# Retention attention and a GELU MLP on one core: first loads reordered, first weight conversions moved behind the chunks' steps, last product split by tokens

## The chip, the cores and the metric

The kernel runs on one core of one Trainium2 chip. The metric is device time in microseconds (us) of one execution. Engines are named as in the profile: PE is TensorE (matmul), PEld its weight loads, DVE is VectorE, ACT is ScalarE, POOL is GpSimd, SP is SyncE, which here only issues DMAs. "L198" is line 198 of the kernel.

## The reference

```python
# retention attention: batch 4, heads 8, 768 steps, head_dim 64
for t in range(S):
    state = gamma[None, :, None, None] * state + np.einsum('bhd,bhe->bhde', k[:, :, t], v[:, :, t])
    y[:, :, t] = scale * np.einsum('bhd,bhde->bhe', q[:, :, t], state)
# bridge: x is y as 3072 tokens x 512
h = x @ w_in                                   # 512 -> 2048
g = h * (1.0 / (1.0 + np.exp(-1.702 * h)))     # quick GELU
return (g @ w_out).astype(np.float32)          # 2048 -> 512
```

The two weight matrices are float64. They reach the chip as raw 64-bit words, and the kernel itself turns them into float32.

## The kernel before

The sequence is cut into 24 chunks of 128 tokens. A chunk goes through three steps: `turn` (transpose q and k on TensorE, copy the result out of PSUM on ScalarE), `attend` (scores on TensorE, mask on VectorE) and `finish` (output and state on TensorE, scaling into `X` on VectorE, decay of the state on GpSimd). The order of TensorE's instructions is the program's. A scheduler sets the order on the other engines, but every engine takes its own instructions one after the other: in the profile, ScalarE began L188 at 40.41 behind L308 at 39.92, as in the program.

Weights come in pieces of 512 KB, and two pieces make the block of one product. `narrow()` converts weights: one pass of ScalarE, then six passes of VectorE. Its first two calls convert one piece each, which together are the first block; every later call converts the two pieces of a whole block.

```python
    def narrow():
        ...
        tc.keep_in_program_order(act.activation(m, hi.bitcast(F32), AF.Abs, scale=2.0 ** 16))          # L188
        tc.keep_in_program_order(dve.tensor_scalar(m, m, F64_MOST * 2.0 ** 16, F64_LEAST * 2.0 ** 16,
                                                   op0=ALU.min, op1=ALU.max))                          # L189
        dve.tensor_scalar(mu, mu, 3, None, op0=ALU.logical_shift_left)                                 # L191
        dve.scalar_tensor_tensor(hi, hi, 0x80000000, mu, op0=ALU.bitwise_and, op1=ALU.bitwise_or)      # L192
        dve.tensor_scalar(mu, hi, 0xFF800000, None, op0=ALU.bitwise_and)                               # L193
        dve.scalar_tensor_tensor(lo.bitcast(F32), lo, 2.0 ** -52, m, op0=ALU.mult, op1=ALU.mult)       # L194
        ...
        dve.tensor_add(w, hi, lo)                                                                      # L198
```

`up0(half, p)` is one product of the MLP's first layer: 8 matmuls into one PSUM tile (16 matmul records in the profile, two for each), then a sigmoid on ScalarE and a multiplication on VectorE. `up0(0, 0)`, `up0(0, 1)` and `up0(0, 2)` are called the first, second and third product below. The third has one more product of the same form directly behind it, with nothing between, so the profile shows the two as one stretch, and I time them as one.

```python
    def hidden(g, h):
        act.activation(s, h, AF.Sigmoid, scale=1.702)       # L308
        ...
            dve.tensor_mul(g, h[:, i], s[:, i])             # L310

    def up0(half, p, tag):
        h = ps.tile([P, 2, TH], F32, name="ph", tag=tag)
        for ab in range(2):
            for c in range(4):
                w = W1[:, p, 2 * ab + c // 2, c % 2, :]
                pe.matmul(h[:, ab], w, X[:, 2 * half + c // 2, c % 2, :], ...)      # L329
        ...  # hidden(...)
```

The start of the program:

```python
    load(0)
    ...
    first = const.tile([P, 1], F32, name="first")
    dve.memset(first, 0.0)
    act.activation(first, first, AF.Sigmoid)     # brings ScalarE's table in early
    fetch()                                      # first weight piece
    load(1)
    fetch()
    ...
    for j in range(CB):                          # CB = 4
        attend(j)
        narrow()
        if j == 1:
            narrow()
        turn(j + 1)
        if j == 0:
            for _ in range(2):
                fetch()
        if j < CB - 1:
            attend(None, j)                      # finish(j)
        else:
            attend(j + 1, j)
        if j:
            up0(0, j - 1, "x")
    ...                                          # the long up stage: 13 products more, narrow() after every other
```

The last product of the last block of tokens is 16 matmuls into one PSUM tile (32 records), an add on VectorE (L423) and one store of 256 KB (L424).

Of the kernel before, what the change touches and what calls it, by code (L numbers as in the profile page):

```python
# [9 lines left out]
F32 = mybir.dt.float32  # L10
U32 = mybir.dt.uint32
AF = mybir.ActivationFunctionType
ALU = mybir.AluOpType
P = 128
# [14 lines left out]
def kernel(  # L29
# [29 lines left out]
    pe, act, dve, pool, sp = nc.tensor, nc.scalar, nc.vector, nc.gpsimd, nc.sync  # L59
# [11 lines left out]
    NB = NCH // CB  # L71
    NFF = DFF // P
    NP = NFF // 2
    C4 = 32
    EH = DM // 2
# [13 lines left out]
    W2 = const.tile([P, 7, NP, EH], F32, name="W2")  # L89
# [16 lines left out]
    def load(j, what="qkv"):  # L106


        b, c = divmod(j, NC)
        rows = slice(c * P, (c + 1) * P)  # L110

        def plain(name, src, tag, bufs, pairs=False, engine=sp):
            t = two.tile([P, H, D], F32, name=name + "_in", tag=tag, bufs=bufs)
            QKV[name, j] = t
            src = src[b, :, rows, :].rearrange("h p d -> p h d")
            if pairs:
                for i in range(2):
                    engine.dma_start(t[:, i:H:2, :], src[:, i * HP:(i + 1) * HP, :])
            else:
                sp.dma_start(t, src)  # L120

        if j < 2 * CB:
            if "q" in what:
                plain("q", q, "q_sq", 2, True)
                plain("kn", k, "k_sq", 2, True, sp if j else act)
        elif "q" in what:
            for name, src in (("q", q), ("k", k)):
                t = two.tile([P, HP, P // C4, C4], F32, name=name + "_sq")
                for r0 in range(0, P, C4):
                    d0 = r0 % D  # L130
                    for hp in range(HP):
                        tc.keep_in_program_order(sp.dma_start(
                            t[r0:r0 + C4, hp],
                            src[b, hp + HP * (r0 // D), rows, d0:d0 + C4].rearrange("(s p) d -> p s d", p=C4)))
                QKV[name, j] = t
        if "v" in what:
            if j >= 2 * CB and c < NC - 1:
                plain("kn", k, "kn", 1)
            plain("v", v, "v", 2)
# [24 lines left out]
    def narrow():  # L164


        i = narrowed[0]
        if i == len(SRC):
            return
        n = 1 if i < 2 else 2  # L170
        narrowed[0] = i + n
        p, h = i // 2 % NP, i % 2

        if i < 2:
            m = W1[:, 1, 2 * h:2 * h + 2].rearrange("p s c f -> p (s c f)")
            w = W1[:, 0, h:4:2].rearrange("p ab c f -> p c ab f")
        elif i < NFF:
            m = W1[:, p, 0:4].rearrange("p s c f -> p (s c f)")
            w = W1[:, p, 0:4].rearrange("p (ab h) c f -> p (h c) ab f", ab=2)
        else:  # L180
            m = w = W2[:, 0:4, p]
        x = raw(i, n).rearrange("p (n two) -> p n two", two=2)
        lo, hi = x[:, :, 0], x[:, :, 1]
        if i >= NFF:
            lo, hi = [t.rearrange("p (s e) -> p s e", s=4) for t in (lo, hi)]
        mu = m.bitcast(U32)
# [8 lines that stand above are left out]
        lo, hi = lo.bitcast(F32), hi.bitcast(F32)  # L195
        if i < NFF:
            lo, hi = [t.rearrange("p (c ab f) -> p c ab f", ab=2, f=P) for t in (lo, hi)]
        dve.tensor_add(w, hi, lo)  # L198
        for _ in range(n):
            fetch()  # L200
# [119 lines left out]
    def g1(m, p, s):  # L320
        return g(m, p // 2 * 2, s)[:, p % 2]
# [7 lines that stand above are left out]
                pe.matmul(h[:, ab], w, X[:, 2 * half + c // 2, c % 2, :], start=(ab == 0 and c == 0), stop=(c == 3),  # L329
                          skip_group_check=True)  # L330
        if half == 0:
            hidden(W1[:, p, 4:6].rearrange("p s c f -> p s (c f)"), h)
        else:
            hidden([(g1(0, p, 2 + i), i) for i in range(2)], h)
# [77 lines left out]
    def down(m):  # L412

        acc, kept = {}, {}
        rows = out[m * BT:(m + 1) * BT, :].rearrange("(h t p) (e c) -> h e p t c", h=2, p=P, c=EH)

        def keep(name, tag, src):
            kept[name] = one.tile([P, 2, EH], F32, name=name, tag=tag)
            act.activation(kept[name], src, AF.Copy)  # L419

        def put(th, e, a, b):
            o = two.tile([P, 2, EH], F32, name="o")
            dve.tensor_add(o, a, b)  # L423
            (pool if m < NB - 1 else act).dma_start(rows[th, e], o)  # L424

        def part(key, sa, sb, new, last, d, then):
            if d == 0 and new:
                acc[key] = ps.tile([P, 2, EH], F32, name="pd", tag=key[0])
            p0 = acc[key]
            for p in range(2 * d, 2 * d + 2):  # L430
                for n in range(2):
                    pe.matmul(p0[:, n, :], g1(m, p, sa)[:, n * P:(n + 1) * P], W2[:, sb, p, :],  # L432
                              start=(new and p == 0 and n == 0), stop=(last and p == NP - 1), skip_group_check=True)
            if d == NP // 2 - 1:
                then(p0)

        def then_p5(y):
            kept["t"] = one.tile([P, 2, EH], F32, name="t", tag="s1")
            dve.tensor_add(kept["t"], y, kept["u"])

        def then_p7(x):
            keep("vv", "s3", x)
            put(1, 0, acc["y1"], kept["vv"])
            put(1, 1, acc["y2"], kept["vv"])

        P_ = [("x", 0, 0, True, False, lambda x: keep("p1", "s1", x)),
              ("y0", 1, 2, True, True, lambda y: put(0, 0, y, kept["p1"])),
              ("y1", 3, 1, True, True, lambda y: None),
              ("x", 0, 5, False, False, lambda x: keep("u", "s2", x)),
              ("y2", 3, 4, True, True, then_p5),  # L450
              ("x", 2, 6, False, True, then_p7),
              ("x2", 1, 3, True, True, lambda y: put(0, 1, y, kept["t"]))]
        todo = []
        for n, (key, sa, sb, new, last, then) in enumerate(P_):
            for d in range(NP // 2):
                def unit(key=key, sa=sa, sb=sb, new=new, last=last, d=d, then=then, n=n):
                    part(key, sa, sb, new, last, d, then)
                    if n == 2:
                        sums_g(m, 2 * d)
                todo.append(unit)  # L460
        return todo


    load(0)
    make_identity(nc, ident)
    pool.dma_start(cold, col_decay[:, 0:2 * H])
    for i in range(2):
        pool.dma_start(rowd[i * D:(i + 1) * D], bass.AP(tensor=row_decay.tensor, offset=row_decay.offset + i * P,
                                                        ap=[[0, D], [2 * P, HP], [1, P]]))

    first = const.tile([P, 1], F32, name="first")
    dve.memset(first, 0.0)
    act.activation(first, first, AF.Sigmoid)
    fetch()
    load(1)
    fetch()
    idle = ps.tile([P, HP, P], F32, name="idle", tag="x")

# [14 lines left out]
    def chunks(first, last):  # L493

        return [s for j in range(first, last + 1)
                for s in (lambda j=j: turn(j), lambda j=j: attend(j, j - 1))]
# [12 lines left out]
        fetch()  # L509
    for j in range(CB):  # L510
        attend(j)
        narrow()
        if j == 1:
            narrow()
        turn(j + 1)
        if j == 0:
# [3 lines that stand above are left out]
            attend(None, j)  # L520
        else:
            attend(j + 1, j)
        if j:
            up0(0, j - 1, "x")
    between = chunks(CB + 1, 2 * CB - 1) + [lambda: attend(None, 2 * CB - 1)]
    for n, unit in enumerate([(1, p) for p in range(3)] + [(half, p) for p in range(3, NP) for half in range(2)]):
        up0(*unit, "xxyx"[n % 4])
# [81 lines left out]
```

## Time and profile before

| | before |
|---|---|
| median of the first 3 runs | 703.62 us (702.62 to 704.25) |
| span of the profiled run, mean clock | 701.9 us, 0.991 |
| TensorE busy | 686.3 us |
| idle of TensorE in all | 15.6 us |

The prediction shows the slices, the timelines of start and end and the clock windows. Read from windows of 0.1 us, the granted clock of this profile fell from 1.00 to 0.50 at 10.28, 23.93 and 34.17 us and rose again at 13.69, 27.34 and 37.58. Each half-speed stretch took 3.41 us, and the six times lie multiples of 3.41 us apart, within 0.02. The windows of about 3.4 us are laid on these times, and by phase the prediction means where a gap lies against them. The view it does not show is the table of waits of TensorE (engine, waiting group, what it waited for: us in total, times, longest):

```profile
PE py L284 <- DVE G L263: 2.5, 3, 1.3
PE pt L225 <- DMA q_in<-in_q_dram: 2.5, 3, 2.0
...
PE ph L329 <- DVE W L198: 0.9, 1, 0.9
...
PE pt L225 <- DMA kn_in<-in_k_dram: 0.3, 1, 0.3
```

L198 is the last pass of a conversion; the up products (L329) waited for it once, for 0.9 us. Conversions were ahead of their use.

### The profile page before, as it was taken

The page shows a single profiled execution, that of the slowest core. Times are in us where ns is not written, and L with a number is a line of the kernel's source. Part 1 is how long each engine was busy: PE and PEld are TensorE (multiplying, and loading weights), DVE is VectorE, ACT ScalarE, POOL GpSimd, SP SyncE. Part 2 cuts the span into 40 slices and gives each one's busy share as a digit, 9 for nine tenths or more (in the row PEclk, how much of TensorE's full clock was granted, in tenths as well). Part 3 has the DMA queues.
Part 4 walks back from the last instruction along what each step waited for, and adds up shares of the span by engine and source line. Part 5 has one row for each costly group of instructions (what it writes and reads, how often), then busy time and mean ns, then how long its engine had stood idle before and what let it go on. Part 6 is the DMA issues. An engine that isn't in the chain of part 4 may idle for free.

```text
span 701.9 us, 11046 instructions
## 1 busy us (share of the span) xinstructions
PE 686.3 (98%) x4493; PEld 572.5 (82%) x4493; DVE 361.5 (52%) x521; ACT 125.8 (18%) x197; POOL 129.7 (18%) x126
## 2 busy tenths in 40 slices
PE   6799999999999999999999999999999999999997
PEld 5588885447888888888888888888888888888886
DVE  3989889993711822443742453453345362344241
ACT  3213333311000001331000332000333000233000
POOL 4221000000466404000324000132200143000030
PEclk9899999999999999999999999999999999999999
DMA  9884343421130224200334300324300210000001
GB/s 230 264 231 133 135 136 135 138 35 28 28 65 27 63 46 103 46 1 15 72 62 91 65 1 8 72 45 90 74 0 3 60 30 13 34 1 1 15 1 45
DMA packets 138754, 46.36 MB, mean 66 GB/s; under 512 B 130176, under 2 KB 131216, under 8 KB 138704
## 3 DMA queue, kind: packets, MB, share of 16 engines
q1 hardware_dynamic: 134704, 38.84, 23.2%
q0 software_dynamic: 1856, 5.52, 2.1%
q10 hardware_dynamic: 2144, 1.31, 0.6%
q8 instruction: 35, 0.57, 0.3%
q14 instruction: 15, 0.12, 0.1%
HBM read 39.33 MB, written 6.29 MB: 65 GB/s over the span
## 4 chain that ended last, share of the span: by engine, by line
PE 93%; DVE 5%; DMA 1%; ACT 0%; SPq 0%; issue 0%; ACTq 0%
PE pd L432 39%; PE px L381 16%; PE py L381 12%; PE ph L329 8%; PE ph L342 8%; PE py L284 4%; PE pa L257 3%; PE py L292 1%; PE py L282 1%; DMA q_in<-in_q_dram 1%; DVE W L371 1%; DVE G L371 1%; PE pt L225 1%; DVE G L372 1%; DVE W L372 1%; DVE W L198 0%
## 5 line engine op out<-in xcount | busy, mean ns | idle before, releaser
L432 PE MATMUL pd<-W,G 128*128 128x256 f32 x1120 | 247.4, 381 | 0.4 <-DVE G L372 0.3
L432 PEld LDWEIGHTS pd<-W,G 128*128 128x128 f32 x1120 | 211.4, 190 | 30.4 <-DVE G L372 1.2
L381 PE MATMUL px<-X,W 128*128 128x256 f32 x512 | 119.0, 379 | 0.0
L381 PEld LDWEIGHTS px<-X,W 128*128 128x128 f32 x512 | 97.3, 190 | 13.2
L381 PE MATMUL py<-X,W 128*128 128x256 f32 x384 | 90.7, 379 | 0.0
L381 PEld LDWEIGHTS py<-X,W 128*128 128x128 f32 x384 | 73.0, 190 | 9.9
L263 DVE TENSOR_TENSOR at<-pa,mask 128x512 f32<-128x512 f32 x32 | 21.7, 686 | 79.6 <-PE py L284 70.8
L329 PE MATMUL ph<-X,W 128*128 128x256 f32 x256 | 60.9, 397 | 1.6 <-DVE W L198 0.9
L329 PEld LDWEIGHTS ph<-X,W 128*128 128x128 f32 x256 | 49.9, 199 | 9.7 <-DVE W L198 1.3
L342 PE MATMUL ph<-W,W 128*128 128x512 f32 x128 | 55.1, 592 | 0.0
L244 POOL TENSOR_TENSOR kd<-kn_in,cold 128x512 f32<-128x512 f32 x13 | 13.5, 1038 | 208.9 <-PE py L292 179.4
L342 PEld LDWEIGHTS ph<-W,W 128*128 128x128 f32 x128 | 24.3, 190 | 30.2 <-issue 29.2
L373 POOL TENSOR_TENSOR G<-G 128x512 f32<-128x512 f32 x20 | 29.5, 1480 | 95.0 <-DVE G L372 92.2
L310 DVE TENSOR_TENSOR G<-G,sg 128x512 f32<-128x512 f32 x48 | 33.0, 688 | 13.7 <-ACT sg L308 13.7
L308 ACT ACTIVATE sg<-G 128x512 f32<-128x512 f32 x48 | 30.2, 630 | 51.0 <-DVE G L391 30.7
L424 POOL DMA_DIRECT2D out_dram<-o x20 | 14.9, 744 | 128.5 <-DVE o L423 128.5
L308 ACT ACTIVATE sg<-ph 128x512 f32<-128x512 f32 x32 | 19.1, 597 | 100.6 <-PE ph L329 49.8
L432 PE MATMUL pd<-W,W 128*128 128x256 f32 x160 | 35.8, 381 | 0.4 <-DVE W L372 0.3
L432 PEld LDWEIGHTS pd<-W,W 128*128 128x128 f32 x160 | 30.2, 190 | 5.7 <-DVE W L372 1.2
L391 DVE TENSOR_TENSOR G<-py,p 128x512 f32<-128x512 f32 x16 | 11.1, 691 | 37.8 <-PE py L381 37.8
L419 ACT ACTIVATE u<-pd 128x512 f32<-128x512 f32 x6 | 3.6, 597 | 148.5 <-PE pd L432 148.5
L423 DVE TENSOR_TENSOR o<-pd,vv 128x512 f32<-128x512 f32 x12 | 7.7, 686 | 35.6 <-ACT vv L419 35.6
(102 smaller groups left out, 655.9 us busy)
## 6 DMA issues: line engine op xcount, KB each, us to landing
v_in<-in_v_dram SPq DMA_DIRECT2D x24, 256.0 KB, 3.5
W<-in_moe_w_in_dram SPq DMA_DIRECT2D x12, 512.0 KB, 4.8
W<-in_moe_w_out_dram SPq DMA_DIRECT2D x10, 512.0 KB, 3.7
out_dram<-o POOLq DMA_DIRECT2D x20, 256.0 KB, 2.7
q_sq<-in_q_dram SPq DMA_DIRECT2D x256, 16.0 KB, 1.7
k_sq<-in_k_dram SPq DMA_DIRECT2D x256, 16.0 KB, 1.7
kn_in<-in_k_dram SPq DMA_DIRECT2D x13, 256.0 KB, 3.2
G<-in_moe_w_out_dram SPq DMA_DIRECT2D x6, 512.0 KB, 3.7
```

Source lines behind the costliest of these rows:

```text
L257: pe.matmul(p[t, i, hp, :], kt[r, hp, t], qt[r, hp, :], start=True, stop=True)
L263: dve.tensor_mul(AT[j][:, i], p[:, i], mask[:, i])
L284: pe.matmul(out, vn[:, HP * r + s, :], a[:, r, s, :], start=(not c and s < 2), stop=(s >= 2), skip_group_check=True)
L308: act.activation(s, h, AF.Sigmoid, scale=1.702)
L310: dve.tensor_mul(g, h[:, i], s[:, i])
L329: pe.matmul(h[:, ab], w, X[:, 2 * half + c // 2, c % 2, :], start=(ab == 0 and c == 0), stop=(c == 3), skip_group_check=True)
L342: pe.matmul(h, w, X1[:, c // 2:4:2, c % 2, :], start=(c == 0), stop=(c == 3))
L371: dve.tensor_sub(a[2], a[0], a[2])
L373: pool.tensor_sub(a[1], a[1], a[0])
L381: pe.matmul(acc[:, u, :], W1[:, 2 * d + u, sa, c, :], X[:, sb, c, :], start=(start and u == 0 and c == 0), stop=(stop and c == 1), skip_gr ...
L424: (pool if m < NB - 1 else act).dma_start(rows[th, e], o)
L432: pe.matmul(p0[:, n, :], g1(m, p, sa)[:, n * P:(n + 1) * P], W2[:, sb, p, :], start=(new and p == 0 and n == 0), stop=(last and p == NP - ...
```

## The change

The intent is to shorten start and end. q and k of chunk 1 are requested ahead of the first weight piece. ScalarE's table is loaded before k. The first conversions stand behind the chunks' steps, so that the attention work comes first. The last product is made by halves of tokens, so that the add and store of the first half run under the second.

```diff
+        def last_product(n):
+            if n == 0:
+                acc["x2"] = ps.tile([P, 2, EH], F32, name="pd", tag="x")
+            y = acc["x2"][:, n, :]
+            for p in range(NP):
+                pe.matmul(y, g1(m, p, 1)[:, n * P:(n + 1) * P], W2[:, 3, p, :], start=(n == 0 and p == 0), ...)
+            o = two.tile([P, EH], F32, name="o")
+            dve.tensor_add(o, y, kept["t"][:, n, :])
+            (act, sp)[n].dma_start(rows[0, 1][:, n, :], o)
 ...
+        if m == NB - 1:
+            todo[-NP // 2:] = [lambda n=n: last_product(n) for n in range(2)]
 ...
+    first = const.tile([P, 1], F32, name="first")
+    dve.memset(first, 0.0)
+    act.activation(first, first, AF.Sigmoid)
     load(0)
 ...
-    first = const.tile([P, 1], F32, name="first")
-    dve.memset(first, 0.0)
-    act.activation(first, first, AF.Sigmoid)
+    load(1, "qk")
     fetch()
-    load(1)
+    load(1, "v")
     fetch()
 ...
         attend(j)
-        narrow()
-        if j == 1:
+        if j:
             narrow()
         turn(j + 1)
 ...
         if j:
             up0(0, j - 1, "x")
+        else:
+            narrow()
```

More of the change, by code (lines that the diff above doesn't have):

```diff
@@ L435, in part @@
                 then(p0)
+        def last_product(n):
[3 more added lines that the diff above has]
+            for p in range(NP):
+                pe.matmul(y, g1(m, p, 1)[:, n * P:(n + 1) * P], W2[:, 3, p, :], start=(n == 0 and p == 0),
+                          stop=(p == NP - 1), skip_group_check=True)
+            o = two.tile([P, EH], F32, name="o")
+            dve.tensor_add(o, y, kept["t"][:, n, :])
+            (act, sp)[n].dma_start(rows[0, 1][:, n, :], o)
         def then_p5(y):
```

## The prediction

> **What bounds the kernel now.** I read the busy shares and slices first, then the waits of TensorE, then the timeline of the start and of the end, and last TensorE's busy time in windows of 3.4 us. The slices of the page:
>
> ```profile
> PE   6799999999999999999999999999999999999997
> DVE  3989889993711822443742453453345362344241
> PEclk9899999999999999999999999999999999999999
> ```
>
> TensorE (PE) works 686.3 of 701.9 us. What it lacks is in the first three slices and the last one: the page has no other gap. So only two places can pay, the first 45 us and the tail, and both are what the change touches. The whole sum of idle time is 15.6 us (2.2%), and VectorE (DVE) is as full as TensorE in the start. The timeline of all engines, start:
>
> ```profile
> 10.79 1.09 PE L225 MATMUL pt<-ident,q_in 128*128 128x128 f32 x4 [1.99 <-DMA q_in<-in_q_dram]
> ...
> 22.88 1.17 ACT L188 ACTIVATE W<-W 128x1024 f32<-128x1024 f32 x1 [4.54 <-DVE W L194]
> ...
> 23.63 4.54 PE L329 MATMUL ph<-X,W 128*128 128x256 f32 x12 [0.86 <-DVE W L198]
> ...
> 31.18 1.22 DVE L198 TENSOR_TENSOR W<-W 128x1024 f32<-128x1024 f32 x1
> ...
> 34.80 5.08 PE L329 MATMUL ph<-X,W 128*128 128x256 f32 x16
> ...
> 39.92 0.60 ACT L308 ACTIVATE sg<-ph 128x512 f32<-128x512 f32 x1 [8.95 <-PE ph L329]
> 40.41 1.17 ACT L188 ACTIVATE W<-W 128x1024 f32<-128x1024 f32 x1
> 40.55 0.69 DVE L310 TENSOR_TENSOR W<-ph,sg 128x512 f32<-128x512 f32 x1 [0.49 <-ACT sg L308]
> ...
> 48.48 1.22 DVE L198 TENSOR_TENSOR W<-W 128x1024 f32<-128x1024 f32 x1
> ```
>
> To be seen: the first wait of note, 1.99 us, is for chunk 1's q. Each weight piece is converted by one ScalarE pass (L188) and six VectorE passes (L189 to L198). The conversion of the second block starts at 22.88, **before** TensorE has run the first up product (23.63 to 28.1), and its last pass ends at 32.40, ahead of the second product at 34.80. Conversions run one block ahead of their use. The lines from 39.92 on show a whole block's conversion started *behind* a product: that took from 39.81 (product over) to 49.70 (48.48 + 1.22), 9.89 us.
>
> TensorE in windows of about 3.4 us (columns: window and length, PE, PEld, DVE, ACT, POOL busy, clock, DMA share, GB/s):
>
> ```profile
> 20.60:24.00 3.40, 1.76 (x13) 1.13 (x9) 2.81 (x6) 1.12 (x1) 0.14 (x1) 0.99 0.95 267
> 24.00:27.40 3.40, 3.40 (x10) 2.69 (x9) 3.25 (x3) 0.05 (x1) 1.93 (x2) 0.51 1.01 319
> ```
>
> Where TensorE was busy 1.76 of 3.4 us, the next window ran at a clock of 0.51. The same happened after 1.54 (6.9 to 10.3) and after 1.61 (30.8 to 34.2), not after 2.60 (41.0 to 44.4). Some 1.7 us of idle in a window is thus followed by a half-speed window, which costs up to another 1.7 us.
>
> The tail of the timeline:
>
> ```profile
> 684.75 12.90 PE L432 MATMUL pd<-W,G 128*128 128x256 f32 x59
> 692.13 6.65 ACTq L424 DMA_DIRECT2D out_dram<-o  x3
> 697.69 0.69 DVE L423 TENSOR_TENSOR o<-pd,t 128x512 f32<-128x512 f32 x1 [4.99 <-PE pd L432]
> ```
>
> After the last matmul come a 0.69 us add and a 256 KB store (2.1 us to landing).
>
> [...] L188 at 40.41 follows L308 at 39.92, as in the program. [...] Here the DMA share is 1.02 from 10 to 20 us and 1.00 from 20 to 30, so bytes that move ahead push others back. [...]
>
> **The change part by part**, with the two programs' instruction order on each engine.
>
> 1. *q and k of chunk 1 ahead of the first weight piece.* Chunk 1's q landed at 10.66 (issued 3.59, 7.07 us), v of chunk 0 at 7.5, the 512 KB piece at 9.27. The piece took 9.27 - 7.5 = 1.8 us of the queue; without it in front q lands near 8.9, and k near 9.7 instead of 11.5. Chunk 0's scores end at 8.80, so the 1.99 us wait goes and so does the half clock behind it. Chunk 0 is finished near 12 instead of 14.75, and chunk 1's scores near 13 instead of 15.76. But then chunk 2's q is needed; before, it landed at about 16.0 (TensorE waited until 16.07) with the DMA engines full. The same bytes stand in front of it, so it still lands near 16. Of 2.7 us some 0.3 remain, and a gap of 3 us invites the half clock there (chunk 1's products cold, +0.9).
>
> 2. *ScalarE's table ahead of k.* The built order is first half of k, table load, dummy activation, second half of k: the second half is issued near 2.85 (1.30 + 1.28 of table + 0.2 of activation) instead of 1.35 and, at the 2.9 to 3.8 us that k's halves took, lands near 6.2 instead of 5.1. k's transposes started at 5.96, so this costs about 0.2, hidden by part 1.
>
> 3. *First conversions behind the chunks' steps.* The number of conversions before the long up stage falls from 12 to 11 calls and each is one slot later. VectorE does chunk 0's and 1's scaling first, the first weight block's last pass ends at about 23.5 as before. I put the first up product's end at 27.7 (28.15 before), **-0.5** for parts 1 to 3 so far, with -2.5 to +0.4 possible as the half clock falls. Then comes what I think decides it. In the new order the second block's L188 stands on ScalarE *after* the first product's sigmoid (L308), and its L189 on VectorE after L310 and chunk 2's two mask passes. It cannot start until TensorE ends the first product. From that end: L310 +0.74, two mask passes to +2.6, L189 +2.54, L191 +3.26, L192 +3.99, chunk scaling +5.1, L193 +5.7, state +6.4, L194 +6.75, L198 +7.9 to +9.1 (spacings of the lines at 39.81 to 49.70). The second product starts at +9.15; before, 34.80 - 28.10 = 6.70: **+2.45**. The third block likewise stands behind the second product. Its sequence is exactly the measured one, so the third product starts 9.93 after it; before, 45.75 - 39.81 = 5.94: **+4.0**. Both gaps (5.1 and 4.0 us) trip the half clock. The second product was cold before too; the third, at 45.75, was warm, so **+1.5** (0.9 to 3.4 by phase). From the fourth block on, use comes at least three products later: the conversion ending at 87.73 is needed at 88.96, the one at 96.73 at 98.55. No further wait. One conversion (5.3 us of VectorE) moves into the long up stage; VectorE has 2.1 us idle there at 158 to 161 and 8.86 after 165.6, so it fits.
>
> 4. *Last product by halves of tokens.* TensorE's 32 recorded matmuls stay. The add shrinks from 0.69 to about 0.42 (0.41 to 0.42 is the 128x256 form elsewhere), the last store from 256 to 128 KB (my estimate, -0.2). But the built program lets the second half's first matmul wait for VectorE's count that the first half's add raises (both halves share one PSUM tile): about 0.04 + 0.42 + 0.04 of idle, and 0.15 of refilling (381 ns for one matmul against 216 between starts). Sum about **+0.1**.
>
> Total: -0.5 + 2.45 + 4.0 + 1.5 + 0.1 = +7.5, so 711; I take **710.5** for a chance that the start gains more.
>
> **The rivals.** (a) The transfer was the only limit: the 1.99 us and the cold window behind it go and the gain reaches the end: 700 to 701. For it: TensorE waited there. Against it: a saturated DMA and VectorE's order. (b) Everything in the start is hidden by the DMA and by VectorE, and conversions keep ahead: 703 to 704. Against it: both queues are in order and show the conversion behind the sigmoid. (c) The serial chain above with two cold windows more: 713 to 714. (d) VectorE becomes the bound in the later stages through the moved conversion: +3 on top, 714; against it the 8.86 us.
>
> **Range and chances.** From the sum, the start can take 2.5 more or give nothing, the clock's phase is worth ±2: 706 to 714. Beyond 2% means 717.7 or 689.5; the idle time in all is 15.6, so faster by that is nearly excluded, and slower needs every term at its worst.
>
> **What would show it.** In the new profile: the wait of 1.99 for chunk 1's q gone, one of 2 to 3 us for chunk 2's q near 16; TensorE waiting for L198 about 5 us before the second up product and 4 us before the third; VectorE idle 3 to 6 us before L310, twice, between 22 and 42; cold windows under the second and third product; no new wait between 60 and 180; about 0.5 us of TensorE waiting for the half add at the end. I am wrong if VectorE runs L189 of the second block before L310 of the first product, or if chunk 2's q lands well ahead of 16.

## The result and the profile after

| | before | changed |
|---|---|---|
| median of 6 runs | 703.90 us (702.62 to 704.88) | 712.67 us (710.54 to 716.54) |
| profiled run: span, mean clock | 701.9 us, 0.991 | 714.8 us, 0.983 |
| TensorE busy in it | 686.3 us | 690.6 us |

The ratio is 1.0129, with a 95% interval of 1.0100 to 1.0157. A ratio here is always the mean time of one kernel's fast runs over the mean of the other's in the same rounds, so it is not quite the ratio of the medians in the table. The change made the kernel about 9 us slower, 1.3%. One caution for all that follows: the profiled run of the changed kernel was its slowest of six. The spans of the other five were 708.8 to 711.7 us.

The slices of the changed kernel's page (busy tenths in 40 slices of 17.9 us, then the granted clock):

```profile
PE   6768999999999999999999999999999999999997
...
DVE  4564998999441463345364345274334272344241
...
PEclk9788999999999999999999999999999999999999
```

The loss sits where the change is: TensorE's third and fourth slice fell from 9 and 9 to 6 and 8, the clock with them, and VectorE's second to fourth from 9, 8 and 9 to 5, 6 and 4. The engine that had been full in the start was no longer full, and the start became longer. The last slice is as before.

The table of TensorE's waits of the changed kernel:

```profile
PE ph L329 <- DVE W L198: 11.6, 3, 5.3
...
PE pt L225 <- DMA q_in<-in_q_dram: 2.1, 3, 1.6
PE pt L225 <- DMA kn_in<-in_k_dram: 1.2, 1, 1.2
...
```

Set against the table of before: the waits for q and k together went from 2.8 to 3.3 us, so they moved rather than went; the wait for the conversion's last pass grew from 0.9 to 11.6 us, those for the mask (L263) are gone, and the split tail brought a wait of 0.7 (its line is shown under "The halves alone").

TensorE's timeline of the changed kernel (start, length, instructions; in brackets the idle time before them and what ended it):

```profile
8.97 0.63 PE L225 MATMUL pt<-ident,q_in 128*128 128x128 f32 x4 [0.20 <-DMA q_in<-in_q_dram]
...
14.48 0.63 PE L225 MATMUL pt<-ident,q_in 128*128 128x128 f32 x4 [1.63 <-DMA q_in<-in_q_dram]
16.32 0.63 PE L225 MATMUL pt<-ident,kn_in 128*128 128x128 f32 x4 [1.21 <-DMA kn_in<-in_k_dram]
...
24.85 5.49 PE L329 MATMUL ph<-X,W 128*128 128x256 f32 x12 [2.28 <-DVE W L198]
30.27 1.24 PE L257 MATMUL pa<-G 64*64 64x128 f32 x32
...
40.01 5.80 PE L329 MATMUL ph<-X,W 128*128 128x256 f32 x16 [5.34 <-DVE W L198]
45.74 1.10 PE L257 MATMUL pa<-G 64*64 64x128 f32 x32
...
55.67 9.95 PE L329 MATMUL ph<-X,W 128*128 128x256 f32 x32 [3.93 <-DVE W L198]
65.45 0.60 PE L225 MATMUL pt<-ident,q_in 128*128 128x128 f32 x4
```

Chunk 1's q is indeed early (8.97 instead of 10.79), and chunk 2's q and k then come late (1.63 and 1.21). The three products each wait for L198. The reason stands in the timelines of ScalarE and VectorE, here around the end of the first product at 30.27:

```profile
30.38 0.60 ACT L308 ACTIVATE sg<-ph 128x512 f32<-128x512 f32 x1 [12.74 <-PE ph L329]
30.87 1.17 ACT L188 ACTIVATE W<-W 128x1024 f32<-128x1024 f32 x1
```

```profile
31.00 0.69 DVE L310 TENSOR_TENSOR W<-ph,sg 128x512 f32<-128x512 f32 x1 [6.21 <-ACT sg L308]
31.61 1.28 DVE L263 TENSOR_TENSOR G<-pa,mask 128x512 f32<-128x512 f32 x2
32.81 0.68 DVE L189 TENSOR_SCALAR W<-W 128x1024 f32<-128x1024 f32 x1
...
38.43 1.52 DVE L198 TENSOR_TENSOR W<-W 128x1024 f32<-128x1024 f32 x1
```

L188 is the first pass of the second block's conversion. It stands behind L308, the first product's sigmoid, so ScalarE had been idle for 12.74 us when L308 began, and VectorE for 6.21 when L310 began. Then the conversion ran, its last pass ended at 39.95, and the second product started at 40.01. In the profile before, the same L188 ran at 22.88, ahead of the product.

The clock, in windows of about 3.4 us (window, length, busy time of PE, PEld, DVE, ACT, POOL, granted clock, DMA share, GB/s):

```profile
51.10:54.50 3.40, 0.64 (x20) 0.50 (x15) 3.40 (x6) 0.00 (x0) 0.00 (x0) 1.00 0.39 89
54.50:57.90 3.40, 2.23 (x5) 1.85 (x6) 1.45 (x2) 0.00 (x0) 0.61 (x1) 0.50 0.35 113
57.90:61.30 3.40, 3.40 (x9) 2.70 (x8) 0.00 (x0) 0.00 (x0) 0.00 (x0) 0.50 0.53 195
```

The wait before the third product spreads over two windows, 0.64 and 2.23 us busy of 3.4, and each is followed by a window at half speed. The half-speed stretches of the start, again read from windows of 0.1 us, were 16.94 to 20.36, 23.77 to 30.60, 37.42 to 44.25 and 54.49 to 61.32 us: one of 3.42 and three of 6.83. The third product with the one behind it took 65.45 - 55.67 = 9.78 us; before, 52.76 - 45.75 = 7.01.

Where the 12.9 us between the two profiled spans come from, each term read off TensorE's timelines. "End" means the start of the instruction that follows the product directly.

| stretch | before | changed | difference | predicted |
|---|---|---|---|---|
| start of the span to the end of the first product | 28.10 | 30.27 | +2.17 | -0.5 |
| end of first product to start of second | 6.70 | 9.74 | +3.04 | +2.45 |
| second product itself (half clock) | 5.01 | 5.73 | +0.72 | in the clock term |
| end of second product to start of third | 5.94 | 9.93 | +3.99 | +4.0 |
| third product and the one behind it (half clock) | 7.01 | 9.78 | +2.77 | +1.5 with the row above |
| from there to the end of the span | 649.14 | 649.35 | +0.21 | +0.1 |
| sum | | | +12.9 | +7.5 |

Nothing was lost or gained in between: from chunk 5's q to the copy of `vv` near the end, the two kernels took 638.02 and 638.03 us.

### The profile page after: what moved, and what is told of

Read it like the earlier page. It is cut to its first block, busy times and chain, and to the rows that moved or that the text cites. A ratio compares the mean times of both kernels' runs of the same rounds, so it can differ in the third digit from the quotient of the medians.

```text
span 714.8 us, 11053 instructions
## 1 busy us (share of the span) xinstructions
PE 690.6 (97%) x4493; PEld 575.1 (80%) x4493; DVE 361.9 (51%) x522; ACT 125.5 (18%) x197; POOL 129.1 (18%) x126
## 4 chain that ended last, share of the span: by engine, by line
PE 91%; DVE 6%; DMA 2%; SPq 0%; issue 0%; ACT 0%; DVEq 0%
PE pd L432 37%; PE px L381 15%; PE py L381 12%; PE ph L329 9%; PE ph L342 8%; PE py L284 3%; PE pa L257 3%; PE py L282 1%; PE py L292 1%; DMA q_in<-in_q_dram 1%; DMA kn_in<-in_k_dram 1%; PE pt L225 1%; DVE W L371 1%; DVE G L371 1%; PE pd L443 1%; DVE G L372 1%
## 5 line engine op out<-in xcount | busy, mean ns | idle before, releaser
L432 PE MATMUL pd<-W,G 128*128 128x256 f32 x1088 | 240.5, 381 | 0.4 <-DVE G L372 0.3
L432 PEld LDWEIGHTS pd<-W,G 128*128 128x128 f32 x1088 | 205.2, 190 | 29.7 <-DVE G L372 1.2
L329 PE MATMUL ph<-X,W 128*128 128x256 f32 x256 | 65.4, 417 | 12.3 <-DVE W L198 11.6
L329 PEld LDWEIGHTS ph<-X,W 128*128 128x128 f32 x256 | 52.9, 211 | 21.6 <-DVE W L198 12.2
L263 DVE TENSOR_TENSOR at<-pa,mask 128x512 f32<-128x512 f32 x32 | 21.7, 686 | 76.3 <-PE py L284 70.8
L244 POOL TENSOR_TENSOR kd<-kn_in,cold 128x512 f32<-128x512 f32 x13 | 13.5, 1038 | 209.0 <-PE py L292 180.2
L310 DVE TENSOR_TENSOR G<-G,sg 128x512 f32<-128x512 f32 x48 | 33.1, 689 | 13.7 <-ACT sg L308 13.7
L308 ACT ACTIVATE sg<-ph 128x512 f32<-128x512 f32 x32 | 19.1, 598 | 118.5 <-PE ph L329 74.8
L308 ACT ACTIVATE sg<-G 128x512 f32<-128x512 f32 x48 | 30.3, 630 | 51.0 <-DVE G L391 30.7
```

The costliest lines, as they stand in the source:

```text
L263: dve.tensor_mul(AT[j][:, i], p[:, i], mask[:, i])
L329: pe.matmul(h[:, ab], w, X[:, 2 * half + c // 2, c % 2, :], start=(ab == 0 and c == 0), stop=(c == 3), skip_group_check=True)
L432: pe.matmul(p0[:, n, :], g1(m, p, sa)[:, n * P:(n + 1) * P], W2[:, sb, p, :], start=(new and p == 0 and n == 0), stop=(last and p == NP - ...
```

## The experiments

My theory: the loss comes from part 3 alone. A conversion that stands behind the sigmoid of the product before it, on engines that keep their order, makes a chain of 9 to 10 us from product to product, and the half clock in the gaps adds the rest. The rivals: the loads (parts 1 and 2) put the weight pieces late, so that conversions wait for data; or the tail costs; or the moved conversion overloads VectorE later. The first four kernels ran on one chip (before: 704.09 us median, 702.36 to 705.43, 11 runs).

**The conversions alone.** The kernel before with part 3 of the diff and nothing else.

```diff
-        narrow()
-        if j == 1:
+        if j:
             narrow()
 ...
             up0(0, j - 1, "x")
+        else:
+            narrow()
```

> The kernel before with the move of the conversions alone (loads, table and last product as before). Theory S (the serial chain: the second and third weight block's conversion stands behind the product before it): TensorE waits for L198 about 5 us before the second and 4 us before the third up product, and the time is 711 to 714, that is +7 to +10 over before, nearly all of the loss. Rival L (the moved loads are what costs: pieces and v come late): within 1.5 us of before, 702 to 705.

Measured: 716.99 us (716.12 to 718.07, 4 runs), ratio 1.0192 (1.0171 to 1.0214). That is the whole loss and more than the 711 to 714 that I expected. It waited for L198 three times, 10.9 us in all; two of these waits, in its timeline of TensorE:

```profile
40.42 5.25 PE L329 MATMUL ph<-X,W 128*128 128x256 f32 x16 [5.47 <-DVE W L198]
55.53 9.67 PE L329 MATMUL ph<-X,W 128*128 128x256 f32 x32 [3.93 <-DVE W L198]
```

The loads stood in their old order, and the waits are those of the changed kernel: the chain from product to product was 9.74 and 9.93 us, to the hundredth the changed kernel's. So the loads are not what delays the conversions. The first product, too, ended late here, at 30.68, and the last pass of its own conversion at 25.92 (23.57 before), so that delay comes with the moved conversions as well.

**The loads alone.** The kernel before with parts 1 and 2.

```diff
+    first = const.tile([P, 1], F32, name="first")
+    dve.memset(first, 0.0)
+    act.activation(first, first, AF.Sigmoid)
     load(0)
 ...
+    load(1, "qk")
     fetch()
-    load(1)
+    load(1, "v")
```

> The kernel before with chunk 1's q and k ahead of the first piece and the table load ahead of k's second half alone. Theory S: the wait of 1.99 us for chunk 1's q goes, but ScalarE's abs pass of the first piece still stands ahead of chunk 1's copies, so little is gained; 702.5 to 704.5, within 1 us of before. Rival L: +5 or more, 709 and up. Rival G (the load was the limit and the gain is lost only through the conversions): 699.5 to 701.5.

Measured: 701.72 us (701.58 to 704.20, 6 runs), ratio 0.9976 (0.9960 to 0.9992), a small gain, 0.8 us below the range that I expected. The first product ended at 24.48 instead of 28.10: its second part began 1.9 us earlier, and no half clock fell on it (granted clock 1.00 from 7 to 31 us), which is the other 1.7. But the second started at 33.12, only 1.68 earlier than before. VectorE was busy for all 3.40 us of the window from 27.6 to 31.0: with the loads early and the conversions still ahead, VectorE was full. The wait for chunk 1's q went; a wait of 1.82 for chunk 2's q (0.31 before) and one of 1.75 for the mask (0.49 before; the next one, 1.30, was there before too) took most of its place.

**The halves alone.** The kernel before with part 4.

```diff
+        if m == NB - 1:
+            todo[-NP // 2:] = [lambda n=n: last_product(n) for n in range(2)]
```

> The kernel before with the last product by halves alone. My sum: a wait of 0.66 us of TensorE for the first half's add and a slower restart against a shorter add and a smaller store: +0.2, between -0.1 and +0.5 of before. Rival: the shorter tail is worth 0.5 us or more, below -0.4.

Measured: 703.22 us (702.13 to 704.79, 6 runs), ratio 0.9992 (0.9977 to 1.0008): no difference that these rounds can show. From the copy of `vv` to the end of the span the profile has 11.24 us, against 11.12 before. The line of the second half in its timeline:

```profile
693.54 3.72 PE L443 MATMUL pd<-W,G 128*128 128x256 f32 x16 [0.66 <-DVE o L446]
```

TensorE waited 0.66 us for the add of the first half, so what the shorter last add and store saved was given back.

**One conversion put back.** The changed kernel with one call of `narrow()` again ahead of the first product, and nothing else undone.

```diff
             attend(j + 1, j)
+        if j == 1:
+            narrow()
         if j:
             up0(0, j - 1, "x")
         else:
```

> The changed kernel with one conversion put back, ahead of the first up product, so that conversions run one block ahead again; loads, table and last product stay changed. Theory S: the waits of 5 and 4 us for L198 fall below 1 us and the half clock under the third product goes; 701.5 to 704.5, so 8 to 11 us less than the changed kernel. Rivals L and H (a half clock that comes with any gap in the start, with the wait for chunk 2's q too): still 707 or more.

Measured: 703.96 us (702.33 to 707.35, 6 runs), ratio 1.0005 (0.9983 to 1.0026). Loads, tail and all other moves stayed, and the loss was gone. ScalarE's timeline:

```profile
22.77 1.16 ACT L188 ACTIVATE W<-W 128x1024 f32<-128x1024 f32 x1 [5.44 <-DVE W L194]
29.29 0.60 ACT L308 ACTIVATE sg<-ph 128x512 f32<-128x512 f32 x1 [5.36 <-PE ph L329]
```

L188 of the second block is ahead of the sigmoid again. The second and third product started at 35.62 and 46.09 without a wait for L198. One call in the right place undoes the whole loss against the kernel before. It does not bring back what the loads alone gained (701.72 us on the same chip): the first block's conversion still stood a slot later, the first product waited 2.71 us for its L198, and ended at 29.18 instead of 24.48.

**The gaps filled.** What share is the half clock? The changed kernel with idle TensorE work in the two gaps, 28 and 22 transposes of the identity into a PSUM tile that nobody reads. The order on the other engines is that of the changed kernel. It ran on a second chip, together with the two versions with two tiles further down (before: 703.58 us median, 701.54 to 705.49, 11 runs).

```diff
             attend(j + 1, j)
+        if j > 1:
+            filler = ps.tile([P, HP, P], F32, name="filler", tag="y")
+            for _ in range((28, 22)[j - 2]):
+                pe.transpose(filler[:, 0, :], ident, ident)
```

> The changed kernel with 28 and 22 idle transposes in TensorE's two gaps (5.3 us ahead of the second, 3.9 us ahead of the third up product); the order on all other engines is the same. Theory: the loss is the two waits (6.5 us) plus the half clock that they bring. With the gaps filled the starts of the two products stay where VectorE puts them, but they run at full clock: 707.5 to 710.5, 2.5 to 5 us less than the changed kernel, and the runs lie closer together than the 6 us of the changed kernel. Rival: the clock plays no part and only the chain counts: within 1 us of the changed kernel, 712 to 714. Rival: the clock is nearly the whole loss: 705 or less.

Measured: 711.62 us (709.36 to 712.12, 6 runs), ratio 1.0103 (1.0082 to 1.0124), a miss. The transposes were too few: 2.22 and 1.37 us of the gaps stayed idle, and the second product ran cold all the same (5.34 us); the third ran warm (7.01). The changed kernel did not run on that chip. The experiment was inconclusive on the size, so I repeated it with more.

**More filling, and the changed kernel again.** 44 and 32 transposes, and on the same, third chip the changed kernel without an edit (before there: 703.45 us median, 702.08 to 705.13, 9 runs).

```diff
-            for _ in range((28, 22)[j - 2]):
+            for _ in range((44, 32)[j - 2]):
```

> As with 28 and 22 idle transposes, but 44 and 32, so that nearly the whole of both gaps is filled; there the second product had still run cold (5.41 us) after 2.2 us of idle. If the half clock is part of the loss, the second and third product now take 3.7 and 7.2 us, their starts stay 9.7 and 9.9 us after the end of the product before, and the time is 3 to 5 us below the changed kernel of the same call: 708 to 710.5. If the clock is no part: equal to it. The two waits themselves (6.4 us) can't go by this.

> The changed kernel itself, unaltered, to stand on the same chip beside the filled ones: 710.5 to 716.5 as in its six runs, median near 712.7.

Measured: filled 710.31 us (710.14 to 711.40, 4 runs), ratio 1.0098 (1.0082 to 1.0114); unaltered 715.97 us (714.51 to 716.29, 5 runs), ratio 1.0174 (1.0158 to 1.0190). TensorE's timeline of the filled one:

```profile
39.73 3.72 PE L329 MATMUL ph<-X,W 128*128 128x256 f32 x16 [0.36 <-DVE W L198]
...
53.31 7.17 PE L329 MATMUL ph<-X,W 128*128 128x256 f32 x32 [0.28 <-DVE W L198]
```

The filled kernel lies 5.7 us below the unaltered one, somewhat more than the 3 to 5 expected; the unaltered one lies inside its range, but 3.3 above the median of 712.7 that I expected. Both products of the filled one ran at full speed, in 3.65 and 7.01 us (to the start of what follows). They started 9.77 and 9.93 us after the product before them, as without filling, so the chain's length is not a matter of the clock. The profiles differ by 3.1 (span 709.6 against 712.7): the two products got 1.82 + 2.64 = 4.5 us shorter, and this profile's first product ended 1.3 us later. Filling thus took 4.5 us of half clock away. The kernel before pays 1.36 of these as well, as its second product took 5.01 us; so of the loss against it, the half clock behind the two waits is 3.1 us in the repeat (0.46 + 2.64). The filled profile is still 7.7 us longer than the one before: +3.07 and +3.99 for the two chains, +1.86 for the first product, -1.36 for the second product, which ran cold before and warm here, and 0.1 for the rest. What remains without the half clock in the two gaps is the two chains, 7.06 us, and the later end of the first product.

**The loads with halves in two tiles.** Parts 1, 2 and 4 without part 3 (the conversions stand as before), and each half of the last product in its own PSUM tile; the lines for the tile, against the changed kernel:

```diff
-            if n == 0:
-                acc["x2"] = ps.tile([P, 2, EH], F32, name="pd", tag="x")
-            y = acc["x2"][:, n, :]
+            y = ps.tile([P, 2, EH], F32, name="pd", tag="x")[:, 0, :]
 ...                                             # start=(p == 0) in each half
```

> The kernel before with the moved loads and the last product by halves, each half in a PSUM tile of its own; conversions as before. The 0.66 us wait of the second half for the first half's add goes, so the halves are worth about 0.6 us of tail: 700.2 to 702, some 2 to 3 us below before and 0.3 to 1 below the loads alone. Rival (the wait is on something else than the shared tile): the wait stays and the time is that of the loads alone, 701.7.

Measured: 701.58 us (700.94 to 702.07, 6 runs), ratio 0.9969 (0.9953 to 0.9986). By time alone this is also the rival's 701.7, and the version with one tile and the moved loads ran on another chip; the profile decides. The whole product is one stretch now, and from `vv` to the end of the span it took 10.30 us, 0.94 less than with one tile:

```profile
689.40 7.07 PE L441 MATMUL pd<-W,G 128*128 128x256 f32 x32
```

So with one tile the built program waited 0.66 us for the first half's add; with two there was no wait and the results were right. Whether one tile needs the wait was not shown: no run let the second half start under that add in one tile.

**The same, with the gap before the second product filled.** 13 transposes in chunk 2's `finish`, where TensorE waits for the mask.

```diff
+            if j == 2:
+                fill(13)
```

> The same with 13 idle transposes in TensorE's gap of 3 us before chunk 2's second step, order of all other engines unchanged. If the half clock after that gap (31 to 34.7 us in the run with the loads alone) is what the second up product still pays, 1 to 1.7 us less: 699 to 700.7. Rival: another gap brings the half clock anyway, same as without.

Measured: 699.76 us (699.48 to 704.65, 6 runs), ratio 0.9956 (0.9931 to 0.9981). Five of the six lie between 699.48 and 700.29, below all six of the version without filling. What the filling did is not shown by the profiles, though. The second product in the version without filling, and in this one (where the line number is another):

```profile
34.09 3.72 PE L329 MATMUL ph<-X,W 128*128 128x256 f32 x16
```

```profile
32.56 3.72 PE L337 MATMUL ph<-X,W 128*128 128x256 f32 x16
```

It took 3.65 us to the start of what follows in both (4.32 with the loads alone, 5.01 before), and began 6.44 us after the end of the first product in both. The 1.5 us between these two spans (699.9 and 698.4) arose earlier: the first product ended at 27.65 without filling and at 26.12 with it. In these two profiles there was no half clock for the filling to remove; that it removes one in the other runs is not shown.

**Every gap of the start filled.** The last one with 6 transposes more before the first product and 6 inside it. It ran on the third chip.

```diff
+                if half == p == ab == 0 and c == 2:
+                    fill(6)
 ...
+        if j == 1:
+            fill(6)
```

> The fastest so far (moved loads, halves in two tiles, one gap filled) with 6 idle transposes more ahead of the first up product and 6 within it, where TensorE waits 0.78 and 0.86 us and the first product then ran cold (4.54 us instead of 2.86). If that goes: 1.0 to 1.7 us less than 699.8, 698.0 to 699.2, in most runs. Rival: the wait for chunk 2's q before it brings the half clock anyway, equal to 699.8.

Measured: 699.75 us (699.42 to 699.81, 5 runs), ratio 0.9944 (0.9931 to 0.9956). The mean clock was 0.999 to 1.000 in all its runs and they lie within 0.4 us, so next to no half clock is left in it. Yet it is no faster than the version before it: the rival's number, though not its reason. In its profile the first product ended at 24.91, 1.21 us earlier than in the profile before it, but the second began at 32.13, only 0.43 earlier. VectorE worked from 22.56 (L189 of the second block) to the start of the second product without a gap, so VectorE, not the clock, set that start. Before that, chunk 1's scores had waited 1.62 us for ScalarE, whose copies (L226, at 11.84) stood behind a pass (L188, at 11.27) that had waited 4.13 us for its piece of weights. It is the same pattern in small. Whether moving that one call gains anything was not tried. The last two versions, which are loads and tail without the moved conversions, are the fastest kernels, half a per cent under the kernel before.

## Why the prediction was right or wrong

The direction and the mechanism held, and the size roughly: about +7 us was predicted, +8.8 measured. The median of 712.67 lay inside the range, 2.2 us above the predicted 710.5. That is partly luck: on the third chip the same program had a median of 715.97, outside the range, and in the profile of the table, the slowest run of six, the terms sum to +12.9 instead of +7.5. The two large misses have one sign: the first term and the clock term were both too low.

- **The chain behind the sigmoid (part 3) was right.** The waits before the second and third product were to be about 5 and 4 us, and are 5.34 and 3.93. The third term, +4.0, was measured as +3.99. Taking the spacing of the same passes from a place in the profile before where they already ran in that order was a good way to size it. The conversions alone cost the whole loss, and one call put back removed it.
- **The second chain was 0.6 us short.** +2.45 was predicted, +3.04 measured. The two passes L193 and L198 took 0.93 and 1.52 us where I counted 0.68 and 1.22. In that stretch GpSimd ran its decay passes (L244 from 34.75 to 36.38 and L301 from 37.34 to 38.87), and L301 itself took 1.53 us where 0.73 was seen at 22.79. So each of the two long passes overlapped one of GpSimd's: L193 from 36.00 to 36.38, L198 from 38.43 to 38.87. In the profile before, where GpSimd ran no pass from 25.92 to 34.96 and from 40 to 50, L193 took 0.70 (at 27.77) and 0.68 (at 45.55), and L198 1.22 both times (at 31.18 and 48.48). No experiment moved GpSimd's pass away, so that the overlap is the cause was not shown. The stretch was 9.73 to 9.77 us in five profiles, so it is regular. And it could have been read: the profile before has the very same sequence of passes, with the same two long ones, at 32.91 to 40.06 (lines below this list). From L189's start to L198's end that is 7.15 us; in the changed kernel it is 39.95 - 32.81 = 7.14. Put behind the +2.54 at which the prediction has L189, it gives a start of the second product at about +9.7, as measured.
- **The clock term was too small.** +1.5 was predicted; +3.5 was measured in the profile above (0.72 + 2.77) and +3.1 in the repeat (0.46 + 2.64); the conversions alone have +2.7 (0.17 + 2.49). My step was "so **+1.5** (0.9 to 3.4 by phase)", one cold window more. The wait before the third product reached across two windows, and both were followed by half speed. The high end of the bracket was nearer. The sentence that some 1.7 us of idle in a window is followed by a half-speed window holds for the three windows that it names, but not in all profiles: in that of the halves alone, TensorE was busy for 1.49 us from 8.10 to 11.50, and the next 3.4 us ran at full clock (1.00). So the busy time of a window does not decide alone; what does stays open.
- **The first term was too small.** "I put the first up product's end at 27.7" became 30.27, and 28.65, 27.55 and 29.96 in the three other profiles with the same instructions up to there. So the -0.5 was met once in four; this term moves by 2.7 us between runs of the same instructions, and my bracket (-2.5 to +0.4) lay too low. Chunk 2's q did not land near 16: TensorE had it at 14.48, as its transfer was issued at 8.86 instead of 10.61. That is one of the two signs of being wrong that the prediction names. Its k came at 16.32, and the two waits, 1.63 and 1.21, together fill the 2 to 3 us that were expected for q; chunk 1's output products ran cold behind them (granted clock 0.50 from 16.94 to 20.36). What I left out is that the first block's own conversion hangs on that, too: VectorE had done L191 of its second piece, then stood idle until chunk 1's products were over, because L296 stood ahead of L192, as the lines below this list show. The same pass waited in the conversions alone, with the loads in their old order. The last pass ended at 24.79 instead of the 23.5 that I took over from before.
- **The second half of k was not delayed.** Step 2 had it issued at 2.85, behind the table load. The table load ran from 1.35 to 2.63, and the second half was issued at 1.41, inside that time. k's transposes started at 6.06, against 5.96 before, so of the 0.2 us that I had charged and called hidden at most 0.1 existed.
- **No wait appeared in the long up stage**, as predicted. The 638 us to the copy of `vv` were the same, so the moved conversion was free and rival (d) is out.
- **The tail** cost 0.2 us in the profile instead of 0.1, and nothing that the timed rounds can show. The wait for the first half's add was there, 0.66 against the expected 0.5. VectorE's two idle times before L310 were there as well, 6.21 and 6.52 us against the expected 3 to 6.
- Of the rivals, (c), the chain with two cold windows more, is nearest to what the two profiled runs of the changed kernel show in the gaps (+3.5 and +3.1 where +1.5 was taken); its time of 713 to 714 lies between the two medians. (a) is out for this change, but the loads alone came near to its 700 to 701, with 701.72; (b) is out by the three waits.

VectorE's timeline of the kernel before, for the second chain:

```profile
32.91 0.69 DVE L189 TENSOR_SCALAR W<-W 128x1024 f32<-128x1024 f32 x1
...
38.54 1.52 DVE L198 TENSOR_TENSOR W<-G 128x1024 f32<-128x1024 f32 x1
```

VectorE's timeline of the changed kernel, for the first term:

```profile
18.66 0.41 DVE L191 TENSOR_SCALAR W<-W 128x512 uint32<-128x512 uint32 x1
20.69 0.69 DVE L296 TENSOR_TENSOR X<-py,rowd 128x512 f32<-128x512 f32 x1 [1.62 <-PE py L292]
21.30 1.08 DVE L192 SCALAR_TENSOR_TENSOR W<-W,W 128x512 uint32<-128x512 uint32 x1
```

L192 needs nothing from L296, and still begins only after it, when TensorE has ended chunk 1.

## What to carry to other kernels

On engines that keep their order, ask of each preparing pass behind which other instruction it stands, not only when its data arrive: a conversion placed behind the sigmoid of one product can only begin when that product ends; here ScalarE and VectorE stood idle until then (12.74 and 6.21 us). Keep preparation one block ahead of the matmuls. A gap in TensorE costs its own length, and can cost a half-speed window behind it: here two came with the gap of 3.93 us, and the stretch of products behind it took 2.77 us longer. And when a product is cut into halves so that the add of one runs under the other, look for a wait between them: here it was 0.66 us with one shared PSUM tile, and none with two.
